# A floor of 208 columns under the first matrix product of an expert visit

## The chip, the cores and the metric

The kernel runs on one core of a Trainium2 chip. The metric is the device time of one execution in microseconds (us), given as the median over several runs. The engines are named as in the profile: PE is TensorE with its matrix products, PEld its weight loads, DVE is VectorE, ACT is ScalarE, POOL is GpSimd, SP is the engine that issues most transfers. The granted clock is a share of 2.4 GHz: 1.00 is the upper level and 0.50 the lower one (1.2 GHz).

## The reference

The program computes a linear attention with a random-feature map and then two mixture-of-experts layers on its 2304 output rows of 512 numbers:

```python
logits = x @ w_gate                      # second layer: + modality_bias[modality_id]
e_idx = np.argmax(logits, axis=1)
probs = softmax(logits); gate_w = probs[np.arange(N), e_idx]
for e in range(E):                       # E = 8 experts, D = 512, F = 1024
    mask = e_idx == e                    # first layer: at most 576 rows of an expert are kept
    h = np.maximum(x[mask] @ w1[e], 0.0)
    out[mask] = gate_w[mask, None] * (h @ w2[e])
```

Each row goes to one expert, so the number of rows of an expert is known only when the program runs.

## The kernel before

After the attention, each expert layer is worked off in visits. A visit takes up to 512 rows (tokens) of one expert. `fetch` gathers the rows of a visit into `xrow` by four indirect transfers issued on POOL, 128 rows each. `turn(a)` transposes one block of 128 rows on PE and splits it into a high and a low part (`xTh` on ACT, `xTl` on DVE), so that `xT` holds 512 columns, one for each token. Places without a token are filled from a spare row.

The weights of a visit come by eight transfers of 512 KB on SP into `raw`, and `piece` splits them in the same way: the high part `wh` on ACT, the low part `wl` on DVE or POOL.

The first product is `one(f, n)`: for each of eight blocks `f` of the hidden layer 12 matmuls (four chunks of the contraction, three combinations of high and low parts) with 128x128 weights and `n` columns of tokens, 96 matmuls in a visit. `keep(f)` then empties the PSUM bank: ReLU to `hTh` on ACT, the remainder to `hTl` on DVE, over all 512 columns whatever `n` is. There are four such banks `pa`.

The second product is `two(c, n)`. In the second layer it has 24 matmuls of 512 columns for each block `c` of 128 tokens that holds any, so one block for up to 128 tokens. `out` scales the result into `y`, and `put` scatters it to the output with an indirect transfer on POOL.

How many columns are streamed is chosen at run time among a few built sizes. `products` builds a tree of branches over the sizes in `BUILT` for that visit, and calls the product with the size that fits. Sizes of the first layer end at 208. Those of the second layer's visits end, by visit, at 256 or 128; 208 occurs there once, as the middle size of the fifth visit:

```python
BUILT = (
    [(512, 464, 424), ..., (512, 288, 208)] + [(512, 256, 208)] * 4,
    [(512, 448, 256)] * 3 + [(512, 464, 256), (512, 208, 128)] + [(512, 256, 128)] * 7,
)
```

The order on each engine is the order of the program text (`InOrder`). In a visit of the second layer, PE has the first product of f = 0 to 3, that of f = 4 to 7, the turns 0 and 1 of the next visit, the second product, and the turns 2 and 3. POOL has its `wl` pieces, the puts of the visit and at the very end the gather for the visit after next (`self.fetch(v + 2)`). A branch on the number of visits leads to the code of the last visit, which has no next one.

Of the kernel before, what the change touches and what calls it, by code (L numbers as in the profile page):

```python
# [60 lines left out]
def moe_chain_kernel(ctx, tc, q, k, v, w_phi, wg1, w1a, w2a, modality, wg2, mbias, w1b, w2b, out, cap):  # L61
# [728 lines left out]
    with ExitStack() as mo:  # L790
# [9 lines left out]
        def bank(k, i=None):  # L800
            if i is None:
                i = turn_of[k]
                turn_of[k] += 1
            return banks[k][i % len(banks[k])]
# [32 lines left out]
        class Layer:  # L837
# [69 lines left out]

            def one(self, f, n):

                ph = bank("pa", f)  # L910
                (xh, xl), (wh, wl) = xT, (t.rearrange("p f (c k) -> p f c k", c=4) for t in wgt[0])
                for m, (c, xt, wt) in enumerate((c, xt, wt) for c in range(4) for xt, wt in ((xh, wh), (xl, wh), (xh, wl))):
                    in_order.tensor.matmul(ph[:, 0:n], lhsT=wt[:, f, c, :], rhs=xt[:, c, 0:n], start=(m == 0), stop=(m == 11))
# [385 lines left out]
```

## Time and profile before

| | us |
|---|---|
| median of 3 runs | 895.21 (892.25 to 898.33) |
| the profiled execution | 894.01 |
| its span, first to last instruction | 892.3 |
| PE busy in the span | 776.1 (87%) |
| PE weight loads busy | 672.0 (75%) |
| DVE / ACT / POOL busy | 521.1 / 421.6 / 428.3 |
| mean granted clock of PE | 0.928 |

The busy times are sums over stages with different limits. "Idle before" in a row is the time in which the engine stood still ahead of that instruction, with what ended it; "issue" is a wait for nothing that the profile shows. Durations of matmuls include a modelled end, so that the spacing of two starts says what one costs in a stream.

In what follows the visits of the second layer that end the program are called by their place: the third last (first product from 780.6 us), the second last (from 805.7 us) and the last (from 842.9 us).

### The profile page before, as it was taken

What the parts mean: (1) busy time and instruction counts of PE and PEld (TensorE: products, weight loads), DVE (VectorE), ACT (ScalarE), POOL (GpSimd) and SP (SyncE); (2) the same over time, 40 slices, a digit from 0 to 9 for tenths busy, and PEclk for the clock granted to TensorE, in tenths of its full rate; (3) what the DMA queues carried; (4) which work ended last, traced back from release to release, by engine and by line L of the source; (5) the groups of instructions that cost most, each with busy time, mean ns of one, the idle gap of its engine ahead of it and who ended that gap; (6) DMA issues with size and microseconds to landing.
All of it is one profiled execution on the core that took longest, in us unless ns stands there. A gap on an engine that the chain in (4) does not pass through costs nothing. (4 is left out here: it accounts for less than half of the span.)

```text
span 892.3 us, 15259 instructions
## 1 busy us (share of the span) xinstructions
PE 776.1 (87%) x5170; PEld 672.0 (75%) x5170; DVE 521.1 (58%) x1225; ACT 421.6 (47%) x807; POOL 428.3 (48%) x544
## 2 busy tenths in 40 slices
PE   7889999999929899999988876889699999996690
PEld 5559986589818789999887776757588888896590
DVE  7855687976667346577797784938332333265330
ACT  4547865578434334455446352522333344356431
POOL 4965537755242535463654541602634444456641
PEclk9989999999968999999999896989899999997755
DMA  8847623251032453645537533402762617273420
GB/s 273 268 157 247 225 62 117 56 213 60 3 96 69 172 191 98 216 163 198 191 119 264 166 128 136 157 2 78 245 227 67 219 61 226 69 237 134 135 51 6
DMA packets 70812, 129.44 MB, mean 145 GB/s; under 512 B 16388, under 2 KB 28804, under 8 KB 70660
## 3 DMA queue, kind: packets, MB, share of 16 engines
q1 hardware_dynamic: 60852, 103.33, 34.2%
q0 software_dynamic: 7360, 21.90, 8.5%
q10 hardware_dynamic: 2448, 2.20, 0.8%
q8 instruction: 92, 1.51, 0.7%
q14 instruction: 60, 0.49, 0.2%
HBM read 94.37 MB, written 35.67 MB: 146 GB/s over the span
## 5 line engine op out<-in xcount | busy, mean ns | idle before, releaser
L55 POOL TENSOR_TENSOR wl<-raw,wh 128x512 fp32r<-128x512 f32 x114 | 150.2, 1323 | 173.8 <-ACT wh L55 173.4
L55 PE MATMUL pa<-xTl,wh 128*128 128x512 f32 (+10 forms) x480 | 163.1, 340 | 2.0 <-issue 2.0
L55 PE MATMUL pa<-xTh,wl 128*128 128x512 f32 (+10 forms) x480 | 162.8, 339 | 1.6 <-issue 1.6
L55 PE MATMUL pa<-xTh,wh 128*128 128x512 f32 (+10 forms) x451 | 153.0, 339 | 1.0 <-DVE hTl L55 1.0
L55 ACT CAST wh<-raw 128x512 fp32r<-128x512 f32 x240 | 142.0, 621 | 7.6 <-DMA raw<-in_moe_w_dram 4.9
L55 DVE SCALAR_TENSOR_TENSOR hTl<-pa,hTh 128x512 fp32r<-128x512 f32 x112 | 76.8, 689 | 112.0 <-ACT hTh L55 111.4
L55 ACT ACTIVATE hTh<-pa 128x512 fp32r<-128x512 f32 x112 | 67.3, 601 | 134.1 <-PE pa L55 134.1
L55 DVE TENSOR_TENSOR wl<-raw,wh 128x512 fp32r<-128x512 f32 x121 | 102.5, 857 | 45.4 <-ACT wh L55 45.3
L55 PEld LDWEIGHTS pa<-xTl,wh 128*128 128x128 f32 x480 | 99.1, 206 | 7.4 <-issue 2.2
L55 PEld LDWEIGHTS pa<-xTh,wl 128*128 128x128 f32 x480 | 99.1, 206 | 7.4 <-issue 2.5
L55 PEld LDWEIGHTS pa<-xTh,wh 128*128 128x128 f32 x451 | 92.8, 206 | 5.8 <-DVE hTl L55 1.1
L55 POOL DMA_INDIRECT xrow<-xs,rowi x61 | 64.2, 1053 | 39.5 <-DVE rowi L55 19.1
L55 PE MATMUL pa<-hTh,wl 128*128 128x424 f32 (+7 forms) x256 | 79.0, 308 | 3.4 <-POOL wl L55 3.4
L55 PE MATMUL pa<-hTl,wh 128*128 128x424 f32 (+7 forms) x256 | 78.6, 307 | 0.0
L55 PE MATMUL pa<-hTh,wh 128*128 128x424 f32 (+7 forms) x240 | 73.7, 307 | 0.0
L541 PE MATMUL po<-kv,e 128*128 128x65 f32 x512 | 64.2, 274 | 0.5 <-DVE rank L677 0.5
L55 POOL DMA_INDIRECT out_dram<-y,tokr x28 | 28.5, 1017 | 75.3 <-ACT y L55 32.8
L55 PE MATMUL pa<-wl,hTh 128*128 128x512 f32 x160 | 63.2, 395 | 0.6 <-DVE wl L55 0.6
L55 PE MATMUL pa<-wh,hTl 128*128 128x512 f32 x160 | 63.0, 394 | 0.0
L541 PEld LDWEIGHTS po<-kv,e 128*128 128x128 f32 x512 | 61.0, 192 | 1.5 <-issue 0.8
L55 PE MATMUL pa<-wh,hTh 128*128 128x512 f32 x151 | 59.5, 394 | 0.0
L55 DVE TENSOR_TENSOR xTl<-pt,xTh 128x512 fp32r<-128x512 f32 x60 | 38.5, 680 | 32.1 <-ACT xTh L55 32.1
(307 smaller groups left out, 1548.4 us busy)
## 6 DMA issues: line engine op xcount, KB each, us to landing
raw<-in_moe_w_dram SPq DMA_DIRECT2D x116, 512.0 KB, 5.5
xs<-hrow SPq DMA_DIRECT2D x18, 524.0 KB, 6.1
xs<-y SPq DMA_DIRECT2D x8, 1048.0 KB, 4.3
out_dram<-hrow SPq DMA_DIRECT2D x9, 512.0 KB, 4.8
qk_sb<-in_k_dram SPq DMA_DIRECT2D x16, 256.0 KB, 3.7
v_sb<-in_v_dram SPq DMA_DIRECT2D x16, 256.0 KB, 3.8
qk_sb<-in_q_dram SPq DMA_DIRECT2D x8, 512.0 KB, 3.9
xs<-y SPq DMA_DIRECT2D x2, 1024.0 KB, 5.3
```

The costliest lines, as they stand in the source:

```text
L55: return f(*a, **kw)
L541: nc.tensor.matmul(po[:, j, :], lhsT=e[:, sg, j, :], rhs=kv[:, h, it["b2"], sg, :], start=(sg == 0), stop=(sg == 1))
```

## The change

One line at the head of `one` raises the number of columns to at least 208. The number of matmuls, the weights, the branches and all other functions stay as they are; the columns from 128 to 207 are those of the second block of `xT`, and their results go to parts of the bank that nothing of the output is taken from.

```diff
             def one(self, f, n):
 
+                n = max(n, 208)
                 ph = bank("pa", f)
                 (xh, xl), (wh, wl) = xT, (t.rearrange("p f (c k) -> p f c k", c=4) for t in wgt[0])
```

## Rows read from the trace of the kernel before

**Rows 1.** Groups by shape, whole span, PE: line, operation, shapes, count | busy, mean ns.
```profile
L55 PE MATMUL pa<-xTl,wh 128*128 128x128 f32 x64 | 23.2, 362 | 0.0
...
L55 PE MATMUL pa<-xTl,wh 128*128 128x208 f32 x64 | 18.4, 288 | 0.0
```

**Rows 2.** Stretches: length, then busy time of PE, PEld, DVE, ACT, POOL; clock, DMA, GB/s.
```profile
545.00:552.45 7.45, 7.45 (x48) 7.42 (x48) 2.44 (x4) 3.30 (x6) 1.20 (x1) 0.72 0.03 9
...
780.62:791.33 10.71, 10.71 (x98) 10.70 (x96) 7.15 (x8) 8.44 (x15) 8.26 (x8) 1.00 0.89 290
...
805.66:815.40 9.74, 8.69 (x73) 8.39 (x74) 7.47 (x10) 9.35 (x19) 4.88 (x7) 1.00 0.10 35
815.40:820.40 5.00, 5.00 (x25) 4.93 (x24) 3.60 (x6) 2.21 (x4) 3.53 (x4) 0.50 0.52 181
...
820.00:826.25 6.25, 0.52 (x4) 0.34 (x3) 0.69 (x1) 1.10 (x2) 5.57 (x6) 0.50 0.99 339
...
842.89:863.40 20.51, 20.51 (x97) 20.51 (x97) 7.24 (x11) 7.73 (x14) 11.34 (x11) 0.50 0.29 56
...
848.00:857.00 9.00, 9.00 (x45) 9.00 (x44) 3.08 (x5) 4.35 (x8) 6.28 (x6) 0.50 0.64 123
857.00:870.80 13.80, 13.61 (x55) 11.89 (x55) 3.73 (x7) 3.39 (x8) 2.71 (x3) 0.65 0.01 2
```

**Rows 3.** PE in order of time, last visit of layer one (starts at 545.00): start, duration.
```profile
545.34 0.41 PE L55 MATMUL pa<-xTl,wh 128*128 128x208 f32 x1
545.55 0.41 PE L55 MATMUL pa<-xTh,wl 128*128 128x208 f32 x1
...
549.31 0.28 PE L55 MATMUL pa<-xTh,wl 128*128 128x208 f32 x1
```

**Rows 4.** PE in order of time, second last visit.
```profile
805.83 0.27 PE L55 MATMUL pa<-xTl,wh 128*128 128x128 f32 x1
805.94 0.27 PE L55 MATMUL pa<-xTh,wl 128*128 128x128 f32 x1
...
813.93 0.33 PE L55 MATMUL pa<-xTh,wh 128*128 128x128 f32 x1 [0.99 <-DVE hTl L55]
...
820.11 0.41 PE L55 MATMUL pa<-xTh,wl 128*128 128x128 f32 x1
826.25 1.97 PE L55 MATMUL pt<-ident,xrow 128*128 128x128 f32 x8 [5.73 <-DMA xrow<-xs,rowi]
```

**Rows 5.** POOL in order of time, from the second last visit to the end.
```profile
822.68 1.00 POOL L55 DMA_INDIRECT xrow<-xs,rowi  x1 [0.30 <-issue]
...
852.65 1.30 POOL L53 TENSOR_TENSOR wl<-raw,wh 128x512 fp32r<-128x512 f32 x1
...
881.38 0.98 POOL L55 DMA_INDIRECT out_dram<-y,tokr  x1 [1.86 <-DMA out_dram<-y,tokr]
```

**Rows 6.** PE in order of time, second product of the last visit.
```profile
863.40 0.73 PE L53 MATMUL pa<-wh,hTh 128*128 128x512 f32 x1
...
866.80 0.39 PE L55 MATMUL pa<-wh,hTl 128*128 128x512 f32 x1
...
870.22 0.39 PE L55 MATMUL pa<-wh,hTl 128*128 128x512 f32 x1
```

**Rows 7.** PE in order of time, second token block of the third last visit.
```profile
797.70 0.39 PE L55 MATMUL pa<-wh,hTh 128*128 128x512 f32 x1
...
802.91 0.40 PE L55 MATMUL pa<-wh,hTl 128*128 128x512 f32 x1
```

**Rows 8.** ACT in order of time: second last visit's first banks, last visit's output.
```profile
809.85 0.62 ACT L53 ACTIVATE hTh<-pa 128x512 fp32r<-128x512 f32 x1
...
810.84 0.64 ACT L55 ACTIVATE hTh<-pa 128x512 fp32r<-128x512 f32 x1
...
870.78 2.42 ACT L55 ACTIVATE y<-pa,sdr 128x512 f32<-128x512 f32 x4 [6.04 <-PEq L892]
```

**Rows 9.** Chain that ended last, its final piece: start, us, what.
```profile
847.53 34.83 DMA xrow<-xs,rowi
```

## The prediction

> **What bounds the kernel now.** I read the groups of PE by shape first, to see where the change acts at all. A product of the first kind with 128 columns occurs 64 times for each of the three combinations of parts [rows 1]. That is 192 matmuls, and at 96 a visit just two visits; all other visits already stream 208 columns or more, and nothing changes in them. The odd thing to see is that the wider product is the shorter one in the mean: 288 ns with 208 columns, 362 ns with 128.
>
> Next I read the stretches [rows 2] and the order of time on PE to place these two visits and to find out why. They are the second last (from 805.66 us) and the last (from 842.89 us). The second last runs at the upper clock until 815.40 and at 0.50 afterwards. The last runs its whole first product, 20.51 us, at 0.50, although PE is busy without a gap: a continuous stream of 128 columns did not bring the clock up. With 208 columns it came up: the last visit of layer one began at 545.00 at the lower clock after a wait, and by 549.31 a matmul took 0.28 us in place of 0.41 [rows 3]. The third last visit held 1.00 through 10.71 us of 208 columns [rows 2].
>
> Last I read what waits for PE. In the last visit, all does: the second product follows the first without a gap at 863.40 [rows 6], the output on ACT follows its end at 870.78 [rows 8], and four scatters on POOL follow each other up to 881.38 [rows 5], then the program closes at 892.3. In the second last visit PE itself waits: its first product is over at 820.5, and the turns begin at 826.25, when the gathered rows have come [rows 4].
>
> **The direct cost of 80 more columns.** Matmuls start 0.11 us apart at the upper clock with 128 columns (805.83, 805.94 [rows 4]) and with 208 (10.71 us for 96, 0.1116 each [rows 2]). At the lower clock it is 20.51/96 = 0.2136 with 128 [rows 2] and 0.21 with 208 (545.34, 545.55 [rows 3]). So the added columns cost nothing at either clock; PE's weight loads, busy 10.70 of 10.71 us, fill the same time and hide them. If that cover were gone, the price would be that of the columns, bounded in the second rival. The Trainium skill ("TensorE: Matmul & The Clock Gate", section "Back-to-back issue gap") gives the spacing of matmuls as the columns divided by the clock, with 2.5 ns more when warm; by that, 80 columns cost 67 ns cold and 33 ns warm, 6.4 and 3.2 us in a visit, and the change would lengthen what it touches. The trace does not agree for this pair of widths.
>
> Nothing is issued more or elsewhere: the counts of matmuls, weight loads, transfers and branches are the same. The second block of `xT`, which the product now reads, is turned together with the first, ahead of the preceding second product, so no new wait arises.
>
> **Second last visit.** I expect the clock to stay up past 815.4. The stall at 813.93, for `hTl` on DVE, stays. Then 36 matmuls follow, and their last one starts after 35 x 0.1116 = 3.9 us at 817.8 in place of 820.11 [rows 4]: 2.3 us less on PE. I count this at nothing. What is late next is the gather: POOL issues the last of its four parts at 822.68 [rows 5], behind the scatters of the visit before, which do not wait for this product, and the turns start with its landing at 826.25. PE idles 8.1 us rather than 5.7. Bounds for the stage: if some of it passed through, at most 2.3 us gained; if the clock came up later in the second product, 1 us more at the lower clock costs about 0.5 us (0.227 in place of 0.427 us for each product of 512 columns), so up to 0.7 us lost. I take 0, since the landing has no part in PE's pace.
>
> **Last visit, first product.** Before: 20.51 us [rows 2]. After: the first half as in the visit at 545.00, 48 matmuls in 7.45 us from a cold start [rows 2]; the second half 48 x 0.1116 = 5.36 us. Sum 12.81, gain 7.7 us. The nearest row is that one because it has the same width and the same kind of start, after a wait of some 7 us at a jump to other code. With the rise at 863.40 to 866.80, 3.4 us after the start of a 512-column stream [rows 6], in place of 4.3 us, the gain would be 0.43 us more. If it came twice as late, 8.6 us after the start, it would be 2.1 us less. The engines that empty the banks keep pace: ACT needs 0.99 us for a block (809.85 to 810.84 [rows 8]) and PE 12 x 0.1116 = 1.34 us. The low weight pieces on POOL start at 852.65, behind the gather [rows 5]; four at 1.3 us end by about 857.9, and the last is needed only some 4.5 us after the second product begins, near 860. A stall like that of 0.99 us in the second last visit [rows 4] is the bound for this.
>
> **Last visit, second product.** From 863.40 to the last start 870.22 it takes 6.82 us, the first 3.4 at the lower clock [rows 6]. Warm, the same 24 matmuls take 797.70 to 802.91, 5.21 us [rows 7]. Gain 1.6 us.
>
> **After it** nothing changes: the output, four scatters one behind the other and the close keep their 22 us and slide forward as a whole.
>
> **Sum.** 7.7 + 1.6 = 9.3 us. On the profiled execution that is 894.0 - 9.3 = 884.7 us (span 883.0). That execution lies 1.2 us under the median, so on the median I get 895.2 - 9.3 = 885.9 us. With the bounds, from 9.3 - 2.1 - 1.0 - 0.7 = 5.5 to 9.3 + 0.4 + 2.3 = 12.0 us gained, the case's own range is 883.2 to 889.7; the inner part, 8 to 10.5, is where I expect it.
>
> **Rivals.**
>
> The clock does not come up in the last visit. For it: it stayed down for 20.5 us of unbroken work there. Against it: rows 3 show the same width coming up from the same kind of start. Then only the columns change, at no cost, and the time is 895.2 us. If it comes up in the second half only, the gain is 4.9 + 1.6 = 6.5 us and the time 888.7.
>
> The columns are paid, which is the slower side. Between 208 and 512 columns the spacing grows from 0.1116 to 0.227 us warm and from 0.2136 to 0.427 cold, 0.38 and 0.70 ns a column. Were this the slope below 208 too, and the clock stayed low, 96 products of the last visit would each cost 56 ns more: 5.4 us, 900.6 us. It decides only if the spacing at 208 exceeds that at 128, and rows 2 to 4 show it equal. The Trainium skill's rule on the gap, above, is this mechanism.
>
> The gather for the second last visit lands later, slower as well: eight weight loads of 512 KB run beside it (DMA 0.99 busy, 339 GB/s [rows 2]), and if a faster product released them ahead of it, they could push the turns from 826.25 by as much as 12 us (4.19 MB at that rate), 898 us with the last visit's gain. It decides from 9.3 us of delay on. Against it: the second half of these loads waits for low pieces on POOL that stand behind the gather.
>
> The end hangs on the last gather. The chain puts 847.53 to 882.4 on it [rows 9], and if it took so long, a quicker last visit would bring nothing: 895.2. Against it: its four times 128 rows, 1.07 MB, moved between 848 and 857 (123 GB/s for 9 us [rows 2]), and hardly anything after; the semaphore that ends the chain is more likely that of the scatters.
>
> **How the numbers follow.** The forecast has 0.84: 885.9 us. The clock that stays low has 0.04, half a gain 0.06, the end on the gather 0.03, the two slower rivals 0.03 together. The range, 882.5 to 889.5, holds the inner forecast, most of the half gain and about 1 us for the median's own scatter. About 1%, 9.0 us here, is what a measurement of this kernel can tell from no change. The forecast lies just beyond: I give 0.55 of its 0.84 to more than 9 us, since the row I chose for the rise is the later of the two, and 0.29 to less. With the rivals: faster 0.55, same 0.42, slower 0.03.
>
> **What would show it.** In the changed profile: spacing of 0.11 us in both visits; no fall of the clock at 815; the turns of the second last visit still at about 826, after a longer wait for the gather; the last visit starting at about 843, its matmuls short some 4 us later, its second product from about 855.7 at 0.227 us from the first on. It would be wrong if the first product of the last visit takes over 15 us, or if the turns at 826 move.

## The result and the profile after

The changed kernel takes 886.13 us (median of 16 runs, 881.45 to 892.23) against 894.28 us of the kernel before on the same chip (16 runs, 890.39 to 898.33). The ratio is 0.991, 95% interval [0.989, 0.993], a gain of 8.2 us by the medians; forecast were 9.3 us and 885.9 us. That the time itself was met within 0.2 us is in part luck: the kernel before came out 0.9 us lower over 16 runs than over the three from which I counted, and the gain 1.1 us smaller. The profiled execution took 885.7 us with a span of 884.0 us; that of before took 894.01 us.

The group of 208 columns by shape, of the whole span after (line, operation, shapes, count | busy, mean ns), now holds all that stood in two groups in [rows 1]:

```profile
L55 PE MATMUL pa<-xTl,wh 128*128 128x208 f32 x128 | 37.8, 296 | 0.0
```

The stretches of the two visits after (length, busy time of PE, PEld, DVE, ACT, POOL, then clock, DMA share, GB/s):

```profile
807.64:819.90 12.26, 11.84 (x96) 11.09 (x96) 9.86 (x14) 11.65 (x24) 8.08 (x9) 1.00 0.22 65
...
842.86:849.20 6.34, 6.34 (x30) 6.34 (x31) 1.48 (x3) 1.92 (x4) 4.50 (x5) 0.50 0.03 4
849.20:856.80 7.60, 7.60 (x69) 7.60 (x69) 5.77 (x6) 5.81 (x11) 6.96 (x6) 1.00 0.67 148
842.86:856.80 13.94, 13.94 (x97) 13.94 (x98) 7.25 (x8) 7.74 (x14) 11.46 (x10) 0.77 0.38 82
856.80:862.40 5.60, 5.53 (x25) 4.23 (x23) 3.81 (x6) 1.11 (x2) 1.99 (x3) 1.00 0.01 3
```

They answer to [rows 2]. The clock no longer falls in the first product of the second last visit, and in the last visit it comes up after 6.3 us; before it stayed at 0.50 for all 20.51 us. PE after, in order of time, at the joints of these stages:

```profile
807.64 0.36 PE L53 MATMUL pa<-xTh,wh 128*128 128x208 f32 x1 [1.35 <-ACT wh L55]
...
825.95 1.97 PE L55 MATMUL pt<-ident,xrow 128*128 128x128 f32 x8 [6.12 <-DMA xrow<-xs,rowi]
...
842.86 0.51 PE L53 MATMUL pa<-xTh,wh 128*128 128x208 f32 x1 [8.17 <-issue]
...
849.15 0.35 PE L55 MATMUL pa<-xTh,wl 128*128 128x208 f32 x1
...
856.70 0.41 PE L53 MATMUL pa<-wh,hTh 128*128 128x512 f32 x1
...
861.94 0.39 PE L55 MATMUL pa<-wh,hTl 128*128 128x512 f32 x1
```

From 842.86 to 856.70 the last visit's first product takes 13.84 us in place of 20.51: 6.7 us. Its second product takes 5.24 us to the last start, in place of 6.82 [rows 6]: 1.6 us. Together 8.3 us, as much as the profiled executions differ. The output follows as before, 8.3 us sooner (POOL after, first and last scatter of the last visit, against 881.38 for the last in [rows 5]):

```profile
863.47 1.05 POOL L55 DMA_INDIRECT out_dram<-y,tokr  x1 [3.46 <-ACT y L55]
...
873.07 0.98 POOL L55 DMA_INDIRECT out_dram<-y,tokr  x1 [1.86 <-DMA out_dram<-y,tokr]
```

One coincidence must be read with care. The last visit starts at the same time in both profiles, but the second last began 2.0 us later after (807.64 against 805.66), so it was 2.0 us shorter. The experiments say whether the change did that; the change profiled once more, at the end of the experiments, shows 37.7 us for the second last visit in place of 35.2.

### The profile page after: what moved, and what is told of

Its sections match the earlier page's. It is cut to its first block, busy times and chain, and to the rows that moved or that the text cites. A ratio compares the mean times of both kernels' runs of the same rounds, so it can differ in the third digit from the quotient of the medians.

```text
span 884.0 us, 15259 instructions
## 1 busy us (share of the span) xinstructions
PE 770.5 (87%) x5170; PEld 667.0 (75%) x5170; DVE 525.6 (59%) x1225; ACT 421.7 (48%) x807; POOL 429.5 (49%) x544
## 5 line engine op out<-in xcount | busy, mean ns | idle before, releaser
L55 PE MATMUL pa<-xTh,wl 128*128 128x208 f32 (+9 forms) x480 | 159.2, 332 | 1.0 <-issue 1.0
L55 PE MATMUL pa<-xTl,wh 128*128 128x208 f32 (+9 forms) x480 | 159.5, 332 | 0.0
L55 PE MATMUL pa<-xTh,wh 128*128 128x208 f32 (+9 forms) x451 | 150.2, 333 | 0.3 <-DVE hTl L55 0.3
L55 DVE TENSOR_TENSOR wl<-raw,wh 128x512 fp32r<-128x512 f32 x121 | 105.6, 883 | 44.3 <-ACT wh L55 44.2
L55 PEld LDWEIGHTS pa<-xTh,wl 128*128 128x128 f32 x480 | 95.4, 199 | 6.5 <-issue 1.4
L55 PEld LDWEIGHTS pa<-xTl,wh 128*128 128x128 f32 x480 | 95.6, 199 | 5.3 <-DVE xTl L55 0.4
L55 PEld LDWEIGHTS pa<-xTh,wh 128*128 128x128 f32 x451 | 89.5, 198 | 5.5 <-DVE hTl L55 0.5
```

Source lines behind the costliest of these rows:

```text
L55: return f(*a, **kw)
```

## The experiments

The theory: all of the gain is the last visit's, where the clock comes up; the 80 added columns cost nothing; the second last visit's product is quicker, but what holds that visit up is the landing of the gathered rows. The rivals: the second last visit contributes; the columns count for themselves; the stage has no slack. In all diffs `self.kind` is the kind of the visit, noted at its start.

### The floor in the last visit alone

```diff
-                n = max(n, 208)
+                n = max(n, 208 if self.kind == "last" else 0)
```

> The floor of 208 columns acts in the last visit alone; the second last streams 128 as before. Theory (the gain is the last visit's, the second last's is taken back by its wait for gathered rows): first product of the last visit 13 to 14 us in place of 20.5, its second product 5.3 in place of 6.8, the clock still falls in the second last visit, and the whole gain of the full change is there: ratio 0.990 to 0.992, about 8.2 us. Rival (the second last visit contributes its 2.3 us as well): 6 us, ratio 0.993 to 0.994.

885.45 us, ratio 0.9885 [0.9841, 0.9929]. The whole gain is there: the theory's 0.990 to 0.992 and the change's 0.991 lie in the interval, though the median came out lower than either, and the rival's 0.993 lies just outside. Stretches of this run's second last visit (128 columns) and of its last visit's first half, and PE's rows at the rise:

```profile
816.00:821.00 5.00, 5.00 (x32) 5.00 (x32) 5.00 (x8) 3.07 (x6) 3.41 (x3) 0.65 0.14 39
...
844.86:851.90 7.04, 7.04 (x48) 7.04 (x49) 2.43 (x4) 3.29 (x6) 4.95 (x5) 0.76 0.05 13
```

```profile
847.95 0.41 PE L55 MATMUL pa<-xTh,wl 128*128 128x208 f32 x1
848.16 0.33 PE L55 MATMUL pa<-xTh,wh 128*128 128x208 f32 x1
848.33 0.28 PE L55 MATMUL pa<-xTl,wh 128*128 128x208 f32 x1
```

The clock still falls in the second last visit (mean 0.65 between 816 and 821), and no loss of time shows for it. In the last visit it rose 3.3 us after the start, in place of 6.3.

### The floor in the second last visit alone

```diff
-                n = max(n, 208)
+                n = max(n, 0 if self.kind == "last" else 208)
```

> The floor acts in all visits but the last, so in the second last alone. Theory: the clock stays up through its first product, PE ends it about 2.2 us sooner, waits that much longer for the gathered rows, and the turns begin at the same distance from the gather; time as before, ratio 0.999 to 1.001. Rival (the gain passes through): 2.3 us, ratio 0.997.

896.49 us, ratio 1.0011 [0.9986, 1.0036]; the rival's 0.997 lies outside, and 1.2 us is the most that the interval leaves for this visit. PE in order of time at the end of the second last visit and the start of the last, and a stretch of the last:

```profile
827.92 1.11 PE L55 MATMUL pt<-ident,xrow 128*128 128x128 f32 x4 [7.07 <-DMA xrow<-xs,rowi]
...
847.30 0.45 PE L53 MATMUL pa<-xTh,wh 128*128 128x128 f32 x1 [7.85 <-issue]
```

```profile
847.30:857.58 10.28, 10.28 (x49) 10.28 (x49) 3.27 (x5) 3.31 (x6) 7.79 (x9) 0.50 0.29 63
```

What PE saved became a wait of 7.07 us for the gather, and the last visit ran at 0.50. From the start of the second last visit to that of the last, the profiles with 208 columns in it show 35.2 us (the change), 38.7 (here, from 808.65), 37.3 and 37.7 (two runs below), and those with 128 show 37.2 (before), 37.5 (the run above), 37.3 and 38.9 (the two runs that follow). The two widths overlap (means 37.2 with 208 and 37.7 with 128), so the 2.0 us by which this visit was shorter in the changed kernel's profile are within what one execution differs from another.

### Half of the last visit

```diff
-                n = max(n, 208)
+                n = max(n, 208 if self.kind == "last" and f < 4 else 0)
```

> The floor acts in the last visit for the first four hidden blocks alone; the other four stream 128 columns, so half of the added columns is left out. Theory (the clock is what saves, the columns cost nothing): the clock comes up 4 to 6.5 us after the start, and once up 128 columns run 0.11 us apart; the 5.4 us of the second half are shorter than the 9.7 us for which 128 columns held the upper clock in the second last visit, so the time is that of the full change, ratio 0.990 to 0.992. Rival (the upper clock is lost as soon as the columns shrink): the second half takes 7 to 10 us, ratio 0.994 to 0.998.

886.45 us, ratio 0.9897 [0.9855, 0.9939]. Stretches of this run: the end of the second last visit's first product, and the last visit's second half:

```profile
816.00:820.50 4.50, 4.14 (x36) 3.88 (x35) 4.50 (x7) 3.36 (x7) 2.79 (x3) 1.00 0.09 15
...
852.48:857.80 5.32, 5.32 (x50) 5.32 (x49) 4.72 (x5) 4.46 (x9) 4.72 (x4) 1.00 0.75 164
```

With the clock up, 48 products of 128 columns take 5.32 us, as much as with 208 (5.36 us in the changed kernel, from 851.34 to 856.70). So the saving is the clock and not the width. The first row holds a miss of what I took for granted: here 128 columns kept the upper clock to the end of the second last visit's first product, at 820.5, where it fell at 815.4 before and at about 817.5 in the first experiment. What differed ahead of the fall is the wait for `hTl`, shorter here; the first line is of the first experiment, the second of this run:

```profile
815.74 0.33 PE L55 MATMUL pa<-xTh,wh 128*128 128x128 f32 x1 [0.94 <-DVE hTl L55]
815.71 0.33 PE L55 MATMUL pa<-xTh,wh 128*128 128x128 f32 x1 [0.64 <-DVE hTl L55]
```

```diff
-                n = max(n, 208)
+                n = max(n, 208 if self.kind == "last" and f >= 4 else 0)
```

> The floor acts in the last visit for the last four hidden blocks alone. Theory: the first half takes 10.25 us at the lower clock as before; the second half starts at the lower clock and comes up 4 to 6.5 us later, so it takes 7.4 to 8.7 us in place of 10.24, and the second product runs warm for 1.5 us less; gain 3 to 4.4 us, ratio 0.995 to 0.9965. Rival (the rise is tied to the time since the start of the visit and not to the columns): rise soon after the first half, gain 6 us or more, ratio below 0.9935.

892.59 us, ratio 0.9967 [0.9942, 0.9993], a gain of 3.0 us. The two halves of the last visit's first product:

```profile
848.13:858.40 10.27, 10.27 (x49) 10.27 (x49) 3.27 (x5) 3.31 (x6) 7.67 (x9) 0.50 0.28 60
858.40:866.14 7.74, 7.74 (x50) 7.74 (x50) 3.18 (x5) 4.42 (x8) 3.60 (x3) 0.68 0.38 69
```

PE had been busy without a gap for 10.27 us at 0.50 when the columns grew; the clock came up 4.9 us after that. In this run the rise follows the wider products and not the time since the visit began; with 128 columns throughout it did not come in 20.5 us [rows 2].

### Columns past the cover

```diff
-                n = max(n, 208)
+                n = max(n, 208 if self.kind == "last" else (512 if n == 128 else 0))
```

> As the full change, but where 128 columns were chosen ahead of the last visit, so in the second last, 512 columns stream. Theory (the second last visit has slack up to the gather, and beyond it columns are paid): its first product waits about 2 us for the turns 2 and 3 and takes 96 x 0.227 = 21.8 us, ends some 11.5 us later than with 208 and 5 to 6 us after the gather has landed; the turns begin then and the second product runs warm, about 1 us less; net 4 to 5 us over the full change, 890 to 891 us, ratio 0.994 to 0.996. Rival (the stage has no slack): 11 us more, ratio above 1.002.

889.18 us, ratio 0.9928 [0.9904, 0.9953]. Against the change's 0.991 that is 1.6 us more, with some 3 us of uncertainty: less than the theory's 4 to 5, which the intervals do not exclude. Of its ratios 0.994 and 0.995 lie in the interval, 0.996 does not, and the rival's 1.002 is far outside. PE at the start and at the end of the second last visit's first product, and at the turns 2 and 3:

```profile
804.61 0.50 PE L53 MATMUL pa<-xTh,wh 128*128 128x512 f32 x1 [2.62 <-ACT xTh L55]
...
828.69 1.03 PE L55 MATMUL pt<-ident,xrow 128*128 128x128 f32 x8
...
835.02 1.03 PE L55 MATMUL pt<-ident,xrow 128*128 128x128 f32 x8
```

The product takes 24.1 us in place of 12.3, and the turns follow without a wait: 11.8 us more on PE, plus 1.3 us of later start. Of these 13.1 us, 6.1 to 7.5 (the two profiles of the change) had been spent waiting for the gather, and the turns and the second product behind it take 6.3 us in place of 7.7, since the clock is up from their start. That leaves 4 to 6 us, and the ratios show 1.6; how much of it the program pays stays open within their uncertainty.

```diff
-                n = max(n, 208)
+                n = max(n, (512 if n == 128 else 0) if self.kind == "last" else 208)
```

> As the full change, but the last visit's first product streams 512 columns. Theory (the clock comes up as with 208; past the cover of the weight loads each column costs): 3.4 to 6.3 us at 0.427 a product, then 0.227, so 23.4 to 24.8 us in place of 13.8 with 208 and 20.5 with 128; 10 us over the full change and 2 to 4 us over the kernel before, ratio 1.002 to 1.005. Rival (columns cost nothing as long as the clock is up): ratio 0.990.

896.47 us, ratio 1.0004 [0.997, 1.0037]: 0.2% under the theory's lower end, which lies in the interval, and the rival's 0.990 lies far outside. The last visit's first product, at the lower and at the upper clock:

```profile
847.44:850.60 3.16, 3.16 (x8) 2.48 (x9) 0.00 (x0) 0.00 (x0) 2.29 (x2) 0.50 0.05 8
850.60:870.84 20.24, 20.24 (x90) 16.76 (x89) 7.25 (x11) 7.73 (x14) 8.94 (x8) 1.00 0.26 55
```

The clock came up after 3.2 us, and yet the product takes 23.4 us, 9.6 more than with 208 columns. At the upper clock PE's weight loads are busy 16.76 of 20.24 us here, against all of 7.60 with 208: past their cover the columns are paid. Where the cover ends at the upper clock, the kernel before shows in visits of the first layer, with 240 and 280 columns:

```profile
474.07 0.28 PE L55 MATMUL pa<-xTh,wh 128*128 128x240 f32 x1
...
475.75 0.27 PE L55 MATMUL pa<-xTh,wh 128*128 128x240 f32 x1
```

```profile
432.23 0.29 PE L55 MATMUL pa<-xTl,wh 128*128 128x280 f32 x1
...
438.10 0.29 PE L55 MATMUL pa<-xTh,wl 128*128 128x280 f32 x1
```

These are 15 and 46 spacings: 0.112 us at 240 columns, as at 128 and 208, and 0.128 at 280. The cover ends between the two.

The Trainium skill ("TensorE: Matmul & The Clock Gate", section "HAM oscillation — how this bites in real kernels") advises, for a product of few rows whose bursts of matmuls are parted by waits for DMA, to reorder the loop or to pad the rows to 512 or more. The last visit's first product has no such waits inside it, and padded to 512 it takes no less time than the kernel before (1.0004); here the padding paid up to what the weight loads hide and no further.

### The gather sooner

The wait in the second last visit is the next thing to take away. In the second layer's middle visits the puts of blocks 2 and 3 go to the next visit, so that the gather leaves POOL sooner:

```diff
+                if kind == "last":            # at the start of a visit
+                    for g in held: g()
...
+                if kind is None:              # after self.mine(v, b)
+                    for g in held: g()
...
-                    if l == 1:
+                    if early:                 # l == 1, kind is None, v > 0
+                        self.held.append(lambda c=c: self.put(c, b))
+                    elif l == 1:
                         self.put(c, b)
```

> The full change, and in the second layer's middle visits the puts of blocks 2 and 3 are put off to the next visit, so that POOL issues the gather some 3.3 us sooner. Theory (the second last visit ends with the landing of the gather): its turns begin about 15 us after the start of its first product in place of 18 to 20, and 2.5 to 3.5 us are gained over the full change: ratio 0.986 to 0.989. Rival (another wait takes its place, the low weight pieces on POOL or the start of the last visit's code): ratio 0.990 to 0.992.

886.48 us, ratio 0.9906 [0.9872, 0.9939]: the rival's range, though the theory's 0.988 and 0.989 are not excluded. PE in order of time (the visit began at 802.49), and POOL in the last visit:

```profile
818.22 0.66 PE L55 MATMUL pt<-ident,xrow 128*128 128x128 f32 x4 [0.58 <-DMA xrow<-xs,rowi]
821.00 0.66 PE L55 MATMUL pt<-ident,xrow 128*128 128x128 f32 x4 [2.13 <-DMA xrow<-xs,rowi]
...
856.27 0.79 PE L55 MATMUL pa<-wl,hTh 128*128 128x512 f32 x1 [4.31 <-POOL wl L55]
...
859.42 0.47 PE L55 MATMUL pa<-wh,hTl 128*128 128x512 f32 x1
...
862.27 0.39 PE L55 MATMUL pa<-wh,hTl 128*128 128x512 f32 x1
```

```profile
848.85 1.03 POOL L53 DMA_INDIRECT out_dram<-y,tokr  x1 [0.30 <-issue]
853.92 1.00 POOL L55 DMA_INDIRECT out_dram<-y,tokr  x1 [4.05 <-DMA out_dram<-y,tokr]
854.93 4.97 POOL L55 TENSOR_TENSOR wl<-raw,wh 128x512 fp32r<-128x512 f32 x4
```

The turns begin 15.7 us after the visit's start, as the theory has it. But in the last visit the second held put waits 4.05 us for the first to land, the four low weight pieces stand behind both, and PE's second product waits 4.31 us for them. The wait costs more than its length: PE goes on at the lower clock until 859.4, and from 850.86 to the last start the product takes 11.4 us in place of 5.2. The same order without the floor:

> The earlier gather without the floor of columns. Theory: the gather lands some 4 us sooner, at about 16.5 us after the start of the second last visit's first product, still behind that product's end at 14.9; gain 3 to 4 us over the kernel before, ratio 0.9955 to 0.9965, and the floor is then worth its 8 us on top (ratio to the run with both about 0.991). Rival (with 128 columns and the lower clock PE is late there, so that the second last visit now shows its 2.3 us): ratio 0.998, and the floor worth 10 us on top.

891.83 us, ratio 0.9966 [0.9945, 0.9988], at the theory's upper end: 3.0 us gained. The stretch of its last visit's first product:

```profile
841.84:862.35 20.51, 20.51 (x96) 20.51 (x97) 9.34 (x11) 7.73 (x14) 12.62 (x11) 0.50 0.28 56
```

It takes 20.51 us at 0.50, and PE does not wait for the pieces. So the floor is worth 5.4 us on top of the earlier gather, where 8 or 10 were expected; the intervals leave some 4 us either way, so that 8 is not excluded. In the profiles the quicker last visit runs into a wait of 4.31 us that the slower one does not show.

With the put of block 3 alone held back, and in the last visit behind the pieces, the stall should go:

```diff
-                    if early:
+                    if early and c == 3:
...
-                if kind == "last":            # at the start of a visit
-                    for g in held: g()
...
-                if kind is None:
+                if kind in (None, "last"):
```

> The full change with the earlier gather, but only the put of block 3 is put off, and in the last visit it stands behind the low weight pieces. Theory (with both puts held, the 4.31 us stall of the last visit's second product behind them took the gain): the gather goes out about 2 us sooner than with the full change alone, no stall in the last visit, 2 to 4 us gained over the full change: ratio 0.986 to 0.989. Rival (the second last visit's length is not set by the gather's issue): ratio 0.990 to 0.992.

> The full change once more beside the version with the earlier gather, for a comparison on one chip and a further sample of the clock's rise in the last visit: ratio 0.989 to 0.993; rise 3.3 to 6.3 us after the visit's start; second last visit's start to the last visit's start about 37 us.

886.94 us, 0.9917 [0.9890, 0.9944], against 885.51 us, 0.9908 [0.9877, 0.9938], for the change again. No stall for `wl` is left, yet nothing is gained that these runs can tell. Stretches of the last visit's first product, of the version with the held put:

```profile
838.24:843.00 4.76, 4.76 (x22) 4.76 (x23) 1.09 (x2) 1.10 (x2) 3.48 (x4) 0.50 0.03 7
...
838.24:852.09 13.85, 13.44 (x96) 13.26 (x97) 8.45 (x9) 7.74 (x14) 10.31 (x10) 0.82 0.41 83
```

```profile
850.66 0.37 PE L55 MATMUL pa<-xTh,wh 128*128 128x208 f32 x1 [0.41 <-DVE hTl L55]
```

and of the change again, with PE's rows at the start of the last two visits:

```profile
839.17:843.10 3.93, 3.93 (x18) 3.93 (x19) 0.26 (x1) 0.95 (x2) 2.53 (x4) 0.50 0.03 6
839.17:851.86 12.69, 12.69 (x96) 12.69 (x97) 7.15 (x8) 7.74 (x14) 10.05 (x10) 0.84 0.40 79
```

```profile
801.48 0.36 PE L53 MATMUL pa<-xTh,wh 128*128 128x208 f32 x1 [1.33 <-ACT wh L55]
...
809.94 0.36 PE L55 MATMUL pa<-xTh,wh 128*128 128x208 f32 x1 [0.99 <-DVE hTl L55]
...
839.17 0.51 PE L53 MATMUL pa<-xTh,wh 128*128 128x208 f32 x1 [7.69 <-issue]
```

The second last visit was 35.5 us long with the held put and 37.7 without, but the last visit gave 1.2 us of it back: about 0.5 by a later rise of the clock (5.0 us after the start in place of 3.9, at 0.48 us for each) and 0.4 by a wait for DVE. With intervals of 0.3% either way, whether the earlier gather is worth a microsecond or two beside the floor stays open.

One wait no run tried to shorten: ahead of the last visit PE stands still for 6.9 to 8.2 us in all twelve profiles, for nothing that the profile shows ("issue"), and the visit then starts at 0.50.

## Why the prediction was right, point by point

**Where it acts.** Right: two visits, 192 matmuls.

**The direct cost of nothing.** Right. 96 products of 208 columns filled the second last visit's first product in 12.3 us at clock 1.00, stalls included, and 128 columns at the upper clock took the same 5.3 us a half as 208. The reason given held too: in the last visit PE's weight loads were busy through all 13.94 us, and the spacing grows only past 240 columns. From 208 to 512 the columns do count, 9.6 us in the last visit; the slope that the prediction drew evenly between these two widths begins later. The rule that the prediction took from the Trainium skill ("TensorE: Matmul & The Clock Gate", section "Back-to-back issue gap"), columns divided by the clock, is given there for a single matmul by itself; for a stream in which weight loads and matmuls alternate, as here, the section says that both set the spacing. The prediction left that out, and the trace agrees with it: the spacing is the same at 128 and 208 columns, with the weight loads busy throughout.

**Second last visit, taken at 0.** Right in the sum, within 1.2 us: the floor in it alone gave 1.0011 [0.9986, 1.0036]. Not right in the picture: I expected PE to wait 8.1 us rather than 5.7; the profiles show 6.1 and 7.5 for the change, since the landing of the gather itself moves by 2 us from one execution to the next. The turns at 825.95 and the last visit at 842.86 met the forecast's 826 and 843 by luck: the visit had begun 2.0 us later than before. The wait for `hTl`, 0.99 us before and expected to stay, was 0.32 us in the changed profile and 0.99 in the change again. The fall of the clock there, which I took as a fixed cost of 128 columns, is not one: in one of the five profiles with 128 columns in this visit it did not come within the product.

**Last visit, first product.** The mechanism was right, the size a little off: 6.7 us gained in the profile where the forecast had 7.7. The term that was mis-sized is the time to the rise of the clock, set to 4.3 us after the one row of this kind [rows 3]; in the changed profile it is 6.3. I had held a gain of more than 9 us more likely than less (0.55 to 0.29) because that row was the later of the two at hand; 8.2 us came. Over seven executions in which the last visit started with 208 columns (the change twice, the floor there alone, in its first half, with 512 columns in the second last visit, and both versions with the earlier gather) it is 6.3, 3.9, 3.3, 4.4, 5.6, 4.6 and 5.0, 4.7 in the mean. Each microsecond costs 1 - 0.1116/0.2136 = 0.48 us, so the mean asks for 0.2 us less gain than forecast, and the spread of 3 us moves a run by 1.4 us. The rivals of this step fell: the clock came up, and in the first half of the product (8.5 us, from 842.86 to 851.34) and not only in the second.

**Last visit, second product.** Right: 1.6 us, warm from its first matmul on.

**After it.** Right: from the last product's end to the end of the span it takes as long as before. The rival that the last gather ends the program fell with the change itself: the chain still names it, and the span ended 8.3 us sooner although the gather was issued no sooner (its last part at 851.65, against 851.62).

**The slower rivals** did not come; both visits' spacing is equal at 128 and 208 columns, and the gather was not pushed back.

## What to carry to other kernels

A stream of matmuls that keeps TensorE busy without a gap can still run at the lower clock, here for 20.5 us; read the granted clock of the stretch, and compare the spacing of two widths before paying for the narrower one. Where weight loads set the spacing, wider products are free up to their cover, here somewhere from 240 to 280 columns, and may buy the clock; at 512 columns they were paid with 9.6 us. Price such a gain only where the stage ends on TensorE: of two visits that became quicker on PE, one gave all of it, and of the other's 2.3 us nothing could be measured.

## What had not been expected of the hardware

The time from the start of a stream of 208 columns to the upper clock was not fixed: 3.3 to 6.3 us over seven executions, 6.3 and 3.9 for the change itself. A stream of 128 columns that began at the upper clock lost it 10 to 11 us later in four executions, each time after a wait for `hTl` (0.99, 0.94, 1.17 and 2.52 us), and kept it through 12.9 us in a fifth, where that wait was 0.64 us. With 208 columns the clock held through waits of 0.98 and 0.99 us, but not always: in the first version with the earlier gather, a wait of 1.92 us in the second last visit was followed by a stretch at the lower clock. What decides between these cases no run here separates.

```profile
811.74 0.50 PE L55 MATMUL pa<-xTh,wh 128*128 128x208 f32 x1 [1.92 <-DVE hTl L55]
```

```profile
812.00:815.00 3.00, 3.00 (x15) 3.00 (x15) 2.67 (x5) 0.37 (x1) 2.39 (x3) 0.50 0.94 354
```
